# Attention with beacon tokens and an ELU feed-forward: the whole instruction order planned anew, with longer transfers in the head and ring places counted by rows

## The chip, the cores and the metric

The kernel runs on one core of one Trainium2 chip. The metric is the device time in microseconds (us) of one execution, lower is better.

## The reference

Eight batches of eight heads attend causally over 576 tokens plus 16 beacon tokens that every query sees; the result goes, token by token, through a two-layer feed-forward with an ELU between.

```python
B, H, S, Nb, D = (8, 8, 576, 16, 64)          # q, k, v, beacon_k, beacon_v in float32
k_all = np.concatenate([beacon_k, k], axis=2)
v_all = np.concatenate([beacon_v, v], axis=2)
scores = scale * np.matmul(q, k_all.transpose(0, 1, 3, 2))
causal[:, Nb:] = np.triu(np.ones((S, S), dtype=bool), k=1)
scores = np.where(causal, -1000000000.0, scores)
a = np.exp(scores - scores.max(-1, keepdims=True))
a /= a.sum(-1, keepdims=True) + 1e-09
attn_out = np.matmul(a, v_all)
x = attn_out.transpose(0, 2, 1, 3).reshape(B * S, H * D)   # 4608 x 512
h = x @ w_in                                               # w_in: 512 x 2048
g = np.where(h > 0.0, h, np.exp(np.minimum(h, 0.0)) - 1.0)
out = g @ w_out                                            # w_out: 2048 x 512
```

## The kernel before

The attention is cut into 32 pairs of heads: pair n is heads 2hp and 2hp+1 of batch b, with n = 4b + hp. For a pair, scores are made with keys on the partitions (`sc`, L439), exponentiated by ScalarE into fp16 (`et`, L448), masked on the diagonal blocks by GpSimd (L454), and multiplied with v and a column of ones (`av`, L473). VectorE divides by the sums (L488, L489) into `x`. `x` is transposed into `xT`, a ring of four batches, which the feed-forward reads. The feed-forward runs in tiles of tokens: tiles 0, 1 and 2 have 128, 128 and 256 tokens, tiles 3 to 10 have 512. First matmul `hps` (L529), exponential on ScalarE (`e`, L536), clamp on GpSimd (L540), join on VectorE into `gt` (L549), second matmul `ops` (L563), copy (L569), store on SP's queue.

Queries and keys of batches 0 to 2 come in pairs (`load_pair`, 288 KB each, runs of 2304 bytes), are cast to bf16 (`cast_pair`, L323) and transposed by TensorE (`tr`, L388 and L398). From batch 3 on they come by chunks of up to 128 tokens (`load_tok`, runs of 256 bytes), are cast (`cast_tok`, L346) and transposed by DMA on SP's queue (`turn_tok`, L353); from batch 2 on `x` is transposed by DMA too (`turn_x`, L359). v comes in five chunks per batch (`load_v`, L369), 128 rows in four of them and 80 in the fifth, cast by L373. The weights come in four parts each on GpSimd's queue (`load_w`, L380), cast on the way.

All instructions are written out in an order that a planner decides while the program is built (`Plan.run`). Each operation has an engine, a key, a duration that the author assumes, operations that it depends on, and slots that it takes and gives back (buffers, PSUM banks, places in the rings of the DMA queues). The planner steps through time, and on each engine starts the ready operation of the lowest key whose slots are free; the order in which they start is the order of the program. On the chip only the true dependencies, the buffers and the order on each engine are left: an assumed duration, an assumed ring place or a dependency between planned operations sets no wait by itself. Where PE has nothing ready before planned time 30, the planner puts in a filler, a matmul of a constant (`spare`, L274), which the chip then runs whether or not PE would have waited.

`load` plans a transfer: an issue on SP or ScalarE's queue, and an operation on "DMA" of the assumed duration. `place(b, a)` gives the keys of batch b, `FIRST` the order of the first loads by name, `AT0` and `AT` the keys of the steps of a pair, `PACES` and `LAG` those of the tiles, `DMA_AT` and `TOK` the place and the engine of the token casts, `ON_POOL` the engine of the first pair casts, `W_AFTER` the mask after which each weight part is issued.

Of the kernel before, what the change touches and what calls it, by code (L numbers as in the profile page):

```python
# [26 lines left out]
class Plan:  # L27
# [5 lines left out]
    def add(self, *args, **kw):  # L33
        op = Op(*args, **kw)
        self.ops.append(op)
        return op
# [102 lines left out]
def kernel(  # L139
# [35 lines left out]
    kc_sz = [min(P, SK - P * i) for i in range(NKC)]  # L175
# [32 lines left out]
    def blocks_of(groups):  # L208
# [9 lines left out]
            name=nc.get_next_instruction_name(),  # L218
# [43 lines left out]
    with tc.tile_pool(name="psum", bufs=1, space=bass.MemoryType.PSUM) as psum:  # L262
# [21 lines left out]
        def load(key, dur, fn, deps=(), take=(), issue=0.47, units=1, on="SP"):  # L284
            ring = ["ring" + on] * units
            issue = add(on, key, issue, fn, deps=deps, take=take + ring)
            issues[on].append(issue)
            if "vst" not in take and on + str(key) != "ACT-899":
                issues["st"].append(issue)
            return add("DMA", key, dur, None, deps=[issue], lat=2.0, give=ring, queue=0 if on == "SP" else 2, parts=2 * units)  # L290

        v_issue = {}
        issues = {"SP": [], "ACT": [], "st": []}
        add("SP", -1e6, 0.8, None)
        add("ACT", -1e6, 0.8, None)
# [30 lines left out]
        def rows_of(is_k, c):  # L326
            if not is_k:
                return 0, min(P, S - P * c), P * c
            r0 = NB if c == 0 else 0
            return r0, kc_sz[c] - r0, P * c - NB + r0  # L330
# [240 lines left out]
        def do_store(tt, t4, cols):  # L571
# [2 lines left out]

        SHIFT = [-8.8, -12.16, 3.82, 7.68, 7.37, 15.72, 15.25, 20.7]
        AT = [-49.72, -1.57, -0.78, 0.0, 0.42, 1.22, 1.53, -12.56]
        AT0 = [[-47.18, -49.17, -39.96, -41.23], [-43.3, -38.3, -37.64, -35.42], [-44.55, -19.83, -27.66, -35.41]]
        PACES = [(-18.35, 2.5, 7.99, 12.09), (-6.14, 3.4, 55.13, 1.74), (-8.68, 1.33, 24.3, 1.89), (37.46, 1.31, 15.04, 2.29), (75.69, 1.42, 8.27, 3.74), (111.87, 2.41, 34.18, 1.87)]  # L580
        W_AFTER = [[-52.45, -48.57, -122.34, -273.93], [16.05, 17.94, 11.68, 32.16]]
        DMA_AT = [-284.54, -157.9, 350.32]
        TOK = ("001110", "110000", "010101", "111000", "001000")
        ON_POOL = "11110000"
        X_ON_ACT = "00"
        LAG = 17.42
        URGE = -104.22
        Q_ON_ACT = "01101011"
        FIRST = (
            "q2 v0 k2 q1 v6 v9 k1 q3 k3 b1 v8 q6 q4 v1 q5 v7 v3 v2 k4 q7 k5 v5 v4 k7 k6 ").split()  # L590
        ON_ACT = "01"
        V_ON_ACT = "10011110"

        def place(b, a):
            return 32 * (b - 1) + 8 * a + SHIFT[b]

# [3 lines left out]
        w_at, marks = {}, []  # L600
# [7 lines left out]
        def plan_loads(n):  # L608
            b, hp = divmod(n, HP)
            if hp == 0:  # L610
                got = load(load_key(f"b{b}", place(b, 0) - 31), 0.2, partial(load_bk, b), take=["vst"])
                bk_in[b] = add("POOL", place(b, -0.9), 0.6, partial(cast_bk, b),
                               deps=[got] + last_T.get(b - 2, []), give=["vst"])
                if b == 0:
                    marks.append(bk_in[b])
            gots = []
            for is_k in (True, False):
                key = load_key(("k" if is_k else "q") + str(n), place(b, hp) - 30)
                on = "ACT" if n == 0 and not is_k else "SP"
                gots.append(load(key, 0.8, partial(load_pair, n, is_k), take=["st"] if is_k else [], issue=0.61, on=on))  # L620
            eng, dur, on = {
                "0": ("DVE", 0.9, nc.vector), "1": ("POOL", 1.23, nc.gpsimd), "2": ("ACT", 1.35, nc.scalar),
            }[ON_POOL[n] if n < len(ON_POOL) else "1"]
            qk_in[n] = add(
                eng, place(b, hp + AT[0]), dur, partial(cast_pair, n, on), deps=gots + [last_T.get(("pair", n - 2))], take=["sb"], give=["st"])

        last_T = {}

        def plan_v(b):
            for jc in range(NKC):  # L630
                key = load_key(f"v{NKC * b + jc}", place(b - 1, 1.8 + 0.4 * jc))
                on, eng = QUEUES[V_ON_ACT[b] == "1"]
                got = load(key, 1.22 if b < 3 else 1.45, partial(load_v, b, jc, eng), take=["vst"], issue=1.2 if jc == 0 else 0.6, units=8, on=on,
                           deps=v_issue[b - 1] if b > 1 else ())
                v_issue.setdefault(b, []).append(issues[on][-1])
                v_cast[b, jc] = add(
                    "DVE", place(b, -0.7 + 0.16 * jc), 0.56, partial(cast_v, b, jc),
                    deps=[got] + last_AV.get(b - 2, []), give=["vst"])

        def plan_w(which, f4):  # L640
            after = marks[max(0, min(len(marks) - 1, round(W_AFTER[which][f4])))]
            got = add("POOL", after.key + 0.01, 0.8, partial(load_w, which, f4), deps=[after])
# [7 lines left out]
        def plan_tok(b):  # L650
            turned[b] = []
            for is_k in (True, False):
                for c in range(0, NKC, 2):
                    m = min(2, NKC - c)
                    i = (0 if is_k else 0.5) + c // 2
                    on, eng = QUEUES[ON_ACT[not is_k] == "1"]
                    gots = [load(place(b, 0) - 30 + i + 0.01 * j, 1.45, partial(load_tok, b, is_k, c + j, eng), units=8, on=on,
                                 take=["st"] if j == 0 else [], issue=1.2 if is_k and c + j == 0 else 0.65) for j in range(m)]
                    on_dve = TOK[b - PE_B][3 * (not is_k) + c // 2] == "0"
                    cast = add("DVE" if on_dve else "POOL", place(b, DMA_AT[0]) + i, 0.36 * m if on_dve else 0.53 * m,  # L660
                               partial(cast_tok, b, is_k, c, m, nc.vector if on_dve else nc.gpsimd),
                               deps=gots, take=["sb"], give=["st"])
                    for j in range(m):
                        s = add("SP", place(b, DMA_AT[1]) + i, 1.25, partial(turn_tok, b, is_k, c + j),
                                deps=[cast] + last_SC.get(b - 2, []), take=ring4)
                        turned[b].append(add("DMA", place(b, DMA_AT[1]) + i, 0.75, None, deps=[s],
                                             give=ring4 + (["sb"] if j == m - 1 else []), lat=1.0, parts=8))

        def plan_T2(n, key):
# [4 lines left out]
            last_T.setdefault(b, []).append(T)  # L674
            kA = add("DVE", key + 0.4 - URGE, 0.47, partial(do_copy2, n, 0, 0, nc.vector), deps=[T])
            qB = add("ACT", key + 0.4 - URGE, 0.4, partial(do_copy2, n, 1, 1, nc.scalar), deps=[T])
            qA = add("ACT", key + 0.5 - URGE, 0.45, partial(do_copy2, n, 1, 0, nc.scalar), deps=[kA])
# [20 lines left out]
        def plan_pair(n):  # L698
            b, hp = divmod(n, HP)
            at = lambda a: place(b, hp + a)  # L700
            key = AT0[0][hp] - 4 if b == 0 else at(AT[1])
            ready = plan_T2(n, key) if b == 0 else plan_T(n, key) if b < PE_B else turned[b]
            masked = {}
            SC = None
            steps = [((0,), AT0[0][hp]), ((1, 2), AT0[1][hp]), ((3,), AT0[2][hp])] if b == 0 else \
                [((0, 1), at(AT[2])), ((2, 3), at(AT[3]))]
            for units, key in steps:
# [19 lines left out]
            for r, groups in enumerate([(0,), (1,), (2,)] if b == 0 else [(0,), (1, 2)]):  # L727
                key = AT0[r][hp] + 2.4 if b == 0 else at(AT[4 + r])
                us = [u for g in groups for u in CUT.of_range[g]]
# [9 lines left out]
                if b >= XB:  # L739
                    for blk in blks:  # L740
                        part.setdefault(blk, []).append(normed[-1])
                    if hp == HP - 1:
                        for blk in blks:
                            s = add("SP", at(AT[7]), 1.25, partial(turn_x, b, blk), deps=part.pop(blk), take=ring4)
                            turns.append((b, s))
                            done = add("DMA", at(AT[7]), 0.75, None, deps=[s], give=ring4, lat=1.0, parts=8)
                            last_X.setdefault(b, []).append(done)
# [22 lines left out]
        def plan_tile(p):  # L770
            lo, hi = TILES[p]
            base, pitch1, start2, pitch2 = PACES[p] if p < len(PACES) else (32 * (p - 2) + LAG,) + PACES[-1][1:]
            xs = []
# [61 lines left out]
            plan_w(1, f4)  # L835
        for p in range(NTT):
            plan_tile(p)
        for b, s in turns:
            s.deps += readers.get(b - RING // S, [])
        for line in issues.values():  # L840
# [33 lines left out]
```

## Time and profile before

| what | value |
|---|---|
| three runs | 355.54, 355.71, 358.62 us; median 355.71 |
| the profiled execution | 354.51 us, span 352.8 us |
| TensorE busy | 344.7 us (98%), of it fillers 20.5 us |
| VectorE, ScalarE, GpSimd busy | 206.1, 193.6, 180.3 us |
| HBM read, written | 37.22 MB, 9.44 MB |
| first `hps` matmul | 32.34 us after the span's start |

The span is what the profiler saw from the first to the last instruction; the time of the same execution is 1.7 us longer. Busy time counts overlapping matmuls once, and the mean duration of a single matmul is longer than its pace, as matmuls are pipelined. In the chain of waits each step is followed back to what released it. The profile names lines of the program before; in the changed program they lie some lines lower (L439 becomes L442, L529 becomes L532, L563 becomes L566).

### The profile page before, as it was taken

The page shows a single profiled execution, that of the slowest core. Times are in us where ns is not written, and L with a number is a line of the kernel's source. Part 1 is how long each engine was busy: PE and PEld are TensorE (multiplying, and loading weights), DVE is VectorE, ACT ScalarE, POOL GpSimd, SP SyncE. Part 2 cuts the span into 40 slices and gives each one's busy share as a digit, 9 for nine tenths or more (in the row PEclk, how much of TensorE's full clock was granted, in tenths as well). Part 3 has the DMA queues.
Part 4 walks back from the last instruction along what each step waited for, and adds up shares of the span by engine and source line. Part 5 has one row for each costly group of instructions (what it writes and reads, how often), then busy time and mean ns, then how long its engine had stood idle before and what let it go on. Part 6 is the DMA issues. An engine that isn't in the chain of part 4 may idle for free.

```text
span 352.8 us, 8449 instructions
## 1 busy us (share of the span) xinstructions
PE 344.7 (98%) x3299; PEld 195.6 (55%) x3299; DVE 206.1 (58%) x428; ACT 193.6 (55%) x289; POOL 180.3 (51%) x353
## 2 busy tenths in 40 slices
PE   8999999999999999999999999999999999999996
PEld 5668887545555445545476664554445544444444
DVE  1377797567656458456656665664655555455322
ACT  2576887477556746584586547663477443343200
POOL 5587776367635655375476455463554333434200
PEclk9999999999999999999999999999999999999999
DMA  7999996799996979999999669867750220000112
GB/s 196 261 293 224 200 241 114 214 226 153 184 197 132 209 157 186 152 202 189 138 233 167 146 121 240 151 100 187 111 135 32 59 69 32 31 31 32 46 73 91
DMA packets 139480, 52.55 MB, mean 149 GB/s; under 512 B 127536, under 2 KB 131888, under 8 KB 139440
## 3 DMA queue, kind: packets, MB, share of 16 engines
q1 hardware_dynamic: 87472, 35.55, 47.8%
q10 hardware_dynamic: 47744, 12.26, 18.6%
q0 software_dynamic: 4224, 4.19, 7.2%
q8 instruction: 26, 0.43, 0.5%
q14 instruction: 14, 0.11, 0.1%
HBM read 37.22 MB, written 9.44 MB: 132 GB/s over the span
## 4 chain that ended last, share of the span: by engine, by line
PE 82%; DMA 8%; DVE 2%; POOL 2%; ACT 2%; SPq 2%; issue 1%; ACTq 0%; DVEq 0%; POOLq 0%
PE ops L563 31%; PE hps L529 30%; PE av L473 8%; PE sc L439 7%; DMA st<-in_k_dram 3%; PE spare L274 3%; DMA xT<-x 3%; DMA kT<-st 2%; DVE gt L549 1%; PE tr L388 1%; ACT et L448 1%; ACT e L536 1%; POOL e L540 1%; PE xt L499 1%; POOL et L454 1%
## 5 line engine op out<-in xcount | busy, mean ns | idle before, releaser
L563 PE MATMUL ops<-w_out,gt 128*128 128x512 f16 (+1 forms) x592 | 144.2, 374 | 0.2 <-DVE gt L549 0.2
L529 PE MATMUL hps<-xT,w_in 128*128 128x512 f16 (+2 forms) x768 | 141.6, 326 | 1.5 <-DVE xT L510 0.5
L549 DVE SCALAR_TENSOR_TENSOR gt<-e,hps 128x512 f16<-128x512 f32 x144 | 97.5, 684 | 76.6 <-POOL e L540 76.1
L540 POOL TENSOR_SCALAR e<-e 128x512 f32<-128x512 f32 x144 | 88.6, 619 | 99.8 <-ACT e L536 97.6
L536 ACT ACTIVATE e<-hps 128x512 f32<-128x512 f32 x144 | 85.5, 600 | 92.6 <-PE hps L529 87.9
L448 ACT ACTIVATE et<-sc 128x768 f16<-128x768 f32 (+3 forms) x128 | 103.9, 863 | 35.2 <-PE sc L439 31.0
L529 PEld LDWEIGHTS <-w_in 128*128 128x128 f16 x768 | 67.9, 98 | 56.5 <-issue 3.0
L563 PEld LDWEIGHTS <-gt 128*128 128x128 f16 x592 | 54.1, 98 | 57.3 <-issue 3.0
L454 POOL TENSOR_SCALAR_AFFINE_SELECT et<-et 128x256 f16<-128x256 f16 (+2 forms) x160 | 62.1, 414 | 46.5 <-ACT et L448 42.9
L473 PEld LDWEIGHTS <-et 128*128 128x128 f16 (+1 forms) x960 | 35.9, 97 | 10.7 <-issue 2.0
L569 DVE COPY osb<-ops 128x512 f32<-128x512 f32 (+1 forms) x37 | 25.0, 675 | 25.4 <-PE ops L563 24.4
L473 PE MATMUL av<-v,et 128*128 128x65 f16 (+1 forms) x960 | 39.6, 193 | 0.2
L439 PE MATMUL sc<-qT,kT 64*128 64x80 bf16 (+3 forms) x704 | 35.2, 228 | 0.8 <-ACT et L448 0.8
L489 DVE TENSOR_TENSOR x<-av,rl 128x256 f16<-128x256 f32 (+2 forms) x68 | 32.1, 471 | 2.3
L439 PEld LDWEIGHTS <-kT 64*128 64x128 bf16 x704 | 20.7, 95 | 19.9 <-issue 18.1
L373 DVE CAST v<-vst 128x512 f16<-128x512 f32 (+1 forms) x40 | 21.4, 539 | 4.7 <-DMA vst<-in_v_dram 4.7
L488 DVE RECIPROCAL rl<-av 128x4 f32<-128x4 f32 (+2 forms) x68 | 12.4, 182 | 19.8 <-PE av L473 18.9
L274 PE MATMUL spare<-ones 128*128 128x256 bf16 x115 | 20.5, 301 | 1.7 <-DVE ones L812 1.3
L274 PEld LDWEIGHTS <-ones 128*128 128x128 bf16 x115 | 11.1, 107 | 6.9 <-issue 2.2
L346 DVE CAST st<-st 128x1024 bf16<-128x1024 f32 (+2 forms) x18 | 11.4, 643 | 2.1 <-DMA st<-in_k_dram 1.0
L346 POOL CAST st<-st 128x1024 bf16<-128x1024 f32 (+2 forms) x12 | 10.7, 892 | 3.2 <-DMA st<-in_k_dram 2.8
L323 POOL CAST st<-st 128x1152 bf16<-128x1152 f32 x8 | 9.1, 1142 | 4.9 <-DMA st<-in_q_dram 3.4
(35 smaller groups left out, 67.6 us busy)
## 6 DMA issues: line engine op xcount, KB each, us to landing
out_dram<-osb SPq DMA_DIRECT2D x35, 256.0 KB, 2.7
st<-in_q_dram ACTq DMA_DIRECT2D x20, 256.0 KB, 4.2
vst<-in_v_dram ACTq DMA_DIRECT2D x15, 256.0 KB, 4.3
st<-in_k_dram SPq DMA_DIRECT2D x15, 256.0 KB, 5.0
st<-in_k_dram SPq DMA_DIRECT2D x12, 288.0 KB, 7.0
st<-in_q_dram SPq DMA_DIRECT2D x11, 288.0 KB, 6.9
vst<-in_v_dram SPq DMA_DIRECT2D x9, 256.0 KB, 7.1
w_in<-in_moe_w_in_dram POOLq DMA_DIRECT2D x4, 512.0 KB, 12.8
```

Source lines behind the costliest of these rows:

```text
L274: nc.tensor.matmul(out=spare[:, 0:2 * P], lhsT=ones[:, 0:P], rhs=ones, start=True, stop=True)
L439: nc.tensor.matmul(out=sc[:, h, o:o + w], lhsT=kT[D * h:D * h + D, P * jc:P * jc + P], rhs=qT[D * h:D * h + D, q0:q0 + w], start=True, sto ...
L448: nc.scalar.activation(out=et[:, :, 0:w], in_=scs[n, u][:, :, 0:w], func=AFT.Exp, bias=0.0, scale=float(1.0 / (D ** 0.5)))
L454: nc.gpsimd.affine_select(out=et[:, :, c0:c0 + dw], in_=et[:, :, c0:c0 + dw], compare_op=ALU.is_ge, fill=fill0, base=q0 + NB - P * jc, pat ...
L473: nc.tensor.matmul(out=av[:, c:c + D + 1], lhsT=ets[n, CUT.unit_of[jc, at]][0:m, h, col:col + P], rhs=v16[0:m, jc, 2 * hp + h, 0:D + 1], s ...
L489: nc.vector.tensor_tensor(out=x16s[b % 2][:, blks[0]:blks[0] + nb, P * hp:P * hp + P].rearrange("q i (h d) -> q i h d", d=D), in0=av[:, :, ...
L529: nc.tensor.matmul(out=hps[:, o:o + z - a], lhsT=w_in16[:, cc, P * fc:P * fc + P], rhs=xT[cc][:, a % RING:a % RING + z - a], start=(cc == ...
L536: nc.scalar.activation(out=e, in_=hpss[tt, i], func=AFT.Exp, bias=0.0, scale=1.0)
L540: nc.gpsimd.tensor_scalar(out=e, in0=e, scalar1=1.0, scalar2=0.0, op0=ALU.min, op1=ALU.max)
L549: nc.vector.scalar_tensor_tensor(out=gt, in0=es[tt, i], scalar=1.0, in1=hpss[tt, i], op0=ALU.subtract, op1=ALU.max)
L563: nc.tensor.matmul(out=opss[tt, t4][:, cols], lhsT=gts[tt, fc][:, P * t4:P * (t4 + 1)], rhs=w_out16[:, fc, cols], start=(fc == 0), stop=(f ...
L569: nc.vector.tensor_copy(out=osb[:, slice(*cols)], in_=opss[tt, t4][:, slice(*cols)])
```

## The change

`load` gets a list `held`: issues with a key between that of "w0" (or "w1") and the end of `FIRST`, which later depend on the landing of that part of w_in. The assumed time of a pair's load goes from 0.8 to 0.85 us; that of a v chunk from 1.22 (batches 0 to 2) to 1.38 (batches 0 and 1), of 128 rows. v and token chunks take ring places by rows, one for 16, in place of eight each, and their assumed time is scaled with them. All constants of the order are new, `FIRST` among them.

```diff
         def load(key, dur, fn, deps=(), take=(), issue=0.47, units=1, on="SP"):
             ring = ["ring" + on] * units
             issue = add(on, key, issue, fn, deps=deps, take=take + ring)
+            for f4, name in enumerate(HELD):
+                if FIRST.index(name) - 200 < key < len(FIRST) - 200:
+                    held.append((issue, f4))
...
-        v_issue = {}
+        v_issue, held, HELD = {}, [], ("w0", "w1")
...
-        SHIFT = [-8.8, -12.16, 3.82, 7.68, 7.37, 15.72, 15.25, 20.7]
-        AT = [-49.72, -1.57, -0.78, 0.0, 0.42, 1.22, 1.53, -12.56]
-        AT0 = [[-47.18, -49.17, -39.96, -41.23], [-43.3, -38.3, -37.64, -35.42], [-44.55, -19.83, -27.66, -35.41]]
...
-        W_AFTER = [[-52.45, -48.57, -122.34, -273.93], [16.05, 17.94, 11.68, 32.16]]
-        DMA_AT = [-284.54, -157.9, 350.32]
-        TOK = ("001110", "110000", "010101", "111000", "001000")
-        ON_POOL = "11110000"
+        SHIFT = [-8.11, -12.89, 4.08, 7.5, 6.31, 15.87, 19.09, 18.0]
+        AT = [-41.45, -1.77, -0.78, -0.08, 0.42, 1.22, 2.2, -14.13]
+        AT0 = [[-44.86, -49.35, -43.46, -42.7], [-49.19, -42.15, -37.26, -26.77], [-39.84, -19.1, -39.15, -26.7]]
...
+        W_AFTER = [[-29.08, -80.3, -129.97, -296.72], [21.56, 13.65, 16.79, 29.92]]
+        DMA_AT = [-295.03, -105.94, 339.58]
+        TOK = ("001010", "110101", "100010", "110101", "011111")
+        ON_POOL = "01011101"
...
-        LAG = 17.42
-        URGE = -104.22
-        Q_ON_ACT = "01101011"
+        LAG = 14.59
+        URGE = -56.96
+        Q_ON_ACT = "11100000"
         FIRST = (
-            "q2 v0 k2 q1 v6 v9 k1 q3 k3 b1 v8 q6 q4 v1 q5 v7 v3 v2 k4 q7 k5 v5 v4 k7 k6 ").split()
+            "q2 k2 q1 v6 v9 k1 v0 b1 q3 k3 v8 q5 q6 q4 v1 v7 k4 k7 k5 v5 v3 k6 v2 v4 q7 w0 w1 ").split()
...
-                gots.append(load(key, 0.8, partial(load_pair, n, is_k), take=["st"] if is_k else [], issue=0.61, on=on))
+                gots.append(load(key, 0.85, partial(load_pair, n, is_k), take=["st"] if is_k else [], issue=0.61, on=on))
...
-                got = load(key, 1.22 if b < 3 else 1.45, partial(load_v, b, jc, eng), take=["vst"], issue=1.2 if jc == 0 else 0.6, units=8, on=on,
+                units = kc_sz[jc] // 16
+                got = load(key, (1.38 if b < 2 else 1.45) * units / 8, partial(load_v, b, jc, eng), take=["vst"],
+                           issue=1.2 if jc == 0 else 0.6, units=units, on=on,
                            deps=v_issue[b - 1] if b > 1 else ())
...
-                    gots = [load(place(b, 0) - 30 + i + 0.01 * j, 1.45, partial(load_tok, b, is_k, c + j, eng), units=8, on=on,
+                    units = [sum(rows_of(is_k, c + j)[:2]) // 16 for j in range(m)]
+                    gots = [load(place(b, 0) - 30 + i + 0.01 * j, 1.45 * units[j] / 8, partial(load_tok, b, is_k, c + j, eng), units=units[j], on=on,
...
+        for issue, f4 in held:
+            issue.deps.append(w_at[0, 4 * f4])
```

More of the change, by code (lines that the diff above doesn't have):

```diff
@@ L573, in do_store @@
             nc.sync.dma_start(out=out[row:row + P, slice(*cols)], in_=osbs[tt, t4, cols][:, slice(*cols)])
-        SHIFT = [-8.8, -12.16, 3.82, 7.68, 7.37, 15.72, 15.25, 20.7]
-        AT = [-49.72, -1.57, -0.78, 0.0, 0.42, 1.22, 1.53, -12.56]
-        AT0 = [[-47.18, -49.17, -39.96, -41.23], [-43.3, -38.3, -37.64, -35.42], [-44.55, -19.83, -27.66, -35.41]]
-        PACES = [(-18.35, 2.5, 7.99, 12.09), (-6.14, 3.4, 55.13, 1.74), (-8.68, 1.33, 24.3, 1.89), (37.46, 1.31, 15.04, 2.29), (75.69, 1.42, 8.27, 3.74), (111.87, 2.41, 34.18, 1.87)]
-        W_AFTER = [[-52.45, -48.57, -122.34, -273.93], [16.05, 17.94, 11.68, 32.16]]
-        DMA_AT = [-284.54, -157.9, 350.32]
-        TOK = ("001110", "110000", "010101", "111000", "001000")
-        ON_POOL = "11110000"
+        SHIFT = [-8.11, -12.89, 4.08, 7.5, 6.31, 15.87, 19.09, 18.0]
+        AT = [-41.45, -1.77, -0.78, -0.08, 0.42, 1.22, 2.2, -14.13]
+        AT0 = [[-44.86, -49.35, -43.46, -42.7], [-49.19, -42.15, -37.26, -26.77], [-39.84, -19.1, -39.15, -26.7]]
+        PACES = [(-17.99, 4.96, 8.86, 9.41), (-6.14, -3.44, 56.27, 0.45), (-6.33, 1.33, 19.25, 2.21), (37.29, 1.31, 16.39, 2.29), (75.69, 1.42, 7.84, 3.74), (111.96, 2.41, 34.23, 1.87)]
+        W_AFTER = [[-29.08, -80.3, -129.97, -296.72], [21.56, 13.65, 16.79, 29.92]]
+        DMA_AT = [-295.03, -105.94, 339.58]
+        TOK = ("001010", "110101", "100010", "110101", "011111")
+        ON_POOL = "01011101"
         X_ON_ACT = "00"
-        LAG = 17.42
-        URGE = -104.22
-        Q_ON_ACT = "01101011"
+        LAG = 14.59
+        URGE = -56.96
+        Q_ON_ACT = "11100000"
         FIRST = (
-            "q2 v0 k2 q1 v6 v9 k1 q3 k3 b1 v8 q6 q4 v1 q5 v7 v3 v2 k4 q7 k5 v5 v4 k7 k6 ").split()
+            "q2 k2 q1 v6 v9 k1 v0 b1 q3 k3 v8 q5 q6 q4 v1 v7 k4 k7 k5 v5 v3 k6 v2 v4 q7 w0 w1 ").split()
         ON_ACT = "01"
```

## The prediction

> **What bounds the kernel now.** I read the busy rows first, then the slices, the warm-up matmuls by window, the chain of waits around the two ends of the head and in the middle, and the landing times last.
>
> ```profile
> PE 344.7 (98%) x3299; PEld 195.6 (55%) x3299; DVE 206.1 (58%) x428; ACT 193.6 (55%) x289; POOL 180.3 (51%) x353
> ...
> PEclk9999999999999999999999999999999999999999
> DMA  7999996799996979999999669867750220000112
> ```
>
> TensorE is the bound: 98% busy at full clock, no other engine above 58%. But part of that is filler (`spare`, L274), and it all lies in the first 32 us. Columns below: window, its length, PE busy (count), weight-load busy, clock, DMA share, GB/s.
>
> ```profile
> 0.00:8.00 8.00, 6.03 (x32) 4.13 (x33) 1.00 0.73 191
> 8.00:16.00 8.00, 6.20 (x42) 3.46 (x41) 1.00 1.20 269
> 16.00:24.00 8.00, 4.17 (x24) 1.85 (x22) 1.00 1.19 273
> 24.00:32.00 8.00, 4.08 (x21) 1.66 (x21) 1.00 1.19 229
> ```
>
> Four fifths of the head's PE time is filler while the DMA engines are full: the head waits for data. Its end, and a place in the middle, in the chain of waits (start, us, what):
>
> ```profile
> 31.42 0.67 DVE st L323
> 32.09 0.20 DVE xT L510
> 32.34 1.05 PE hps L529 x16
> ...
> 116.94 1.26 SPq L353
> 118.88 5.50 DMA st<-in_k_dram
> 124.37 1.02 POOL st L346
> 126.71 2.97 DMA kT<-st
> ```
>
> The first MoE matmul starts at 32.34 because VectorE cast a later pair before it copied `xT` (0.54 us of PE idle there). From then on PE works almost without a gap; where the chain leaves PE, it goes through SP's queue and the transposing transfers of keys. In the last 70 us PE runs at its pace:
>
> ```profile
> 293.47 0.86 PE ops L563 x4
> 294.33 1.73 PE hps L529 x8
> 334.05 15.59 PE ops L563 x88
> ```
>
> 216 ns per 512 columns, so nothing is to be had there. From starts in the trace I take start-to-start costs: 216 ns per 512 columns, 33 ns per `av`, 56 ns per transpose, 29 to 66 ns per score matmul, 120 ns per warm filler. Laid end to end, the 3299 matmuls give 332.4 us; the span of 352.8 has 1.3 before the first, 3.4 after the last, and 15.7 of waits and cold clock: 6.7 up to 32.34 and 9.0 after it, nearly all before 275 us. All waits over 0.2 us after the first MoE matmul add up to 4.1 us (0.56 at 105.5, 0.61 at 125.9, 0.56 at 147.2, 0.38 at 175.2, 0.60 at 243.7, five smaller 1.4).
>
> **The change, part by part.** The sum is against the profiled execution, 354.5 us with span 352.8; the median of the runs shown, 355.7, lies 1.2 above, and I add that at the end.
>
> *Work.* Comparing the instruction orders: the same matmuls but for 14 more fillers (129 for 115), the same loads, stores and masks; one cast of a pair and five of token chunks go from VectorE to GpSimd. The last 60 blocks on PE are the same. So the end can move only by when the first MoE matmul starts and by the waits behind it: the useful matmuls ahead of that start are 255 now, 254 before.
>
> *The hold is empty.* `held` collects loads with a key above w0's and below the end of `FIRST`. w0 and w1 stand last in `FIRST`, so the only key between is w1's own, and no `load` has that name. No wait is added: cost 0, nothing queued behind it. The new `dur` and `units` alter only the order that is written out; what the rings hold on the chip stays.
>
> *Head, start.* The first pair's cast moves from GpSimd (1137 ns) to VectorE (748 to 919), idle then: its transposes come about 0.3 earlier. Six fewer cold fillers (28 take 5.67 us, 0.2 each) precede them, 20 more warm ones follow at 0.107 to 0.12. PE stands still perhaps 0.7 us before the transposes, as 22 fillers end at about 5.9 and the cast at 6.6. The row: fillers run at 213 ns until 6.12, then at 109.
>
> By the Trainium skill ("TensorE: Matmul & The Clock Gate", Part 1: The HAM clock gate), the warm-up takes about 3.4 us of busy time on a free-running window, not a count of matmuls; by that rule six fillers fewer save no cold time, and a pause inside the window could even delay the switch, which gives the clock rival below.
>
> *Head, body.* Loads are issued in nearly the same order, so landings should hold: the second key load at 8.79, the third at 14.38, the fourth at 16.01. The last three v loads of batch 0 sit later in ScalarE's queue, behind exponentials, by 0.7 to 2 us; SP's loads fill the engines meanwhile, and their casts are ordered behind norms that come later anyway. If that cover is gone, one v cast (0.54) is added. The four w_in transfers follow the same mask as before, which should be about 0.4 earlier (22.1 for 22.5); the first landed at 30.89, so 30.5. After the last filler come 10+10+2+10+10+10+1+14+1+10 matmuls, 2.5 us by the costs above; before, the fillers ended at 29.84 and 2.5 us with the 0.54 wait followed. The `xT` copy now precedes the next kT copy, so that wait goes: −0.5. At the other end, if every wait stays and fillers only add: 20×0.107−6×0.20=+0.9. Fillers stand where PE waited anyway, so I take −0.1.
>
> *Middle.* Attention of later batches starts earlier. PE work between the last scores of batch b−2, which free the kT buffer, and the first scores of b falls from 41.0 to 38.7 us (b=3), 36.5 to 35.7 (4), 41.0 to 38.4 (5), 53.9 to 46.3 (6), 55.6 to 43.6 (7). The needed transposes landed ahead of their score matmul by 3.7, 0.95, 2.1, 13.8 and 13.5 us, which leaves 1.4, 0.15, −0.5, about 6 and 2. SP issues at 1.25 us each; a wait there holds every later load, store and transpose in its queue. For batches 6 and 7 all ten transposes now run ahead of the x transposes: 12.5 us of issue, no longer broken up. I take +0.5 (bounds 0 to +4).
>
> *Tiles.* PE work from the last `av` a tile needs to its first matmul falls from 12.7 to 9.9 us (tile 4), 11.4 to 9.9 (5), 9.8 to 8.9 (6), 8.6 to 6.9 (8), and is 8.1 for 7.7 (7), 6.0 (9). Tile 6 and tile 8 had no reserve. Key loads ahead of batch 2's x transposes now stand together, so SP should be free earlier there: +0.3 (0 to +1.7). Of the old waits (4.1), which this order rearranges, I take 0.4 as gone (0 to 4.1). The moved casts (0.64 us on DVE, 0.89 on POOL) find engines that are busy half the time; without that, 0.25 each, 1.5 in all.
>
> Here a rule speaks against the change. Row: key loads of 256 KB land in 5.0 us and of 160 KB in 4.9 (medians), while the order now counts the small one at 5/8 of the large.
>
> ```profile
> st<-in_k_dram SPq DMA_DIRECT2D x15, 256.0 KB, 5.0
> ...
> st<-in_k_dram SPq DMA_DIRECT2D x5, 160.0 KB, 4.9
> ```
>
> The Trainium skill ("DMA: Bandwidth & Descriptors", Anatomy of one DMA) fits about 2.0 us fixed plus bytes over 436 GB/s on the GpSimd path; by that the small load saves an estimated 0.2 us, not the planned 0.54. The trace agrees that rows hardly count for landing, not with the size of the figures; the sum by it would be some 0.3 higher for each of batches 3 to 5.
>
> *Sum.* −0.1+0.5+0.3−0.4=+0.3: 354.8 on the profiled execution, 356.0 on the median.
>
> **The rivals.** *Faster: the waits go.* The wait at 32 us (0.5) and the 4.1 us behind it vanish, no new ones come: 355.7−4.6=351.1. For it: they are single events at places that the new order rearranges. Against: every gap of the middle but one shrinks.
>
> *Slower: SP's transposes come late.* Place: the first scores of batches 3, 4, 5 and 7. Landings in the trace run from 2.3 to 6.5 us after issue. If the denser bursts land 1.5 us later than before, the reserves 1.4, 0.15, −0.5 and 0.9 (batch 7's last chunk) turn into waits of 0.1+1.35+2.0+0.6=4.05: 355.7+4.05=359.8. It decides from the point where a transpose lands after PE has arrived. For it: batch 4's was within 1 us before. Against: key loads issued side by side may start the chain earlier.
>
> *Fillers count in full.* Every new filler lengthens the head: +0.9, with the other terms 357.0. For it: PE is busy all through the head. Against: DMA is full there.
>
> *The clock.* The pause before the first transposes puts off the switch: some 15 fillers and 20 small matmuls at half pace, 15×0.104+20×0.056=2.7, of which the data wait hides half: 357.3. It is the rule cited above. Against: 4.7 us of fillers precede the pause.
>
> **How the numbers follow.** Forecast (356.0) 0.55; fillers in full 0.10; clock 0.03; faster 0.13; slower 0.19. One per cent, 3.6 us, is about what a measurement of this kernel can tell from no change; forecast, fillers and clock are within it, so faster 0.13, same 0.68, slower 0.19. The range reaches from short of the faster case to just past the slower one, 352.3 to 360.2; the forecast's own is 354 to 358.
>
> **What would show it.** Right: first MoE matmul between 31.7 and 33.3; 129 fillers; PE busy 97 to 98%; single waits of PE of 0.2 to 1 us at the first scores of batch 4 or 5, behind a transpose. Wrong: the start before 31 or after 34; waits behind transposes above 3 us in sum; or no wait over 0.3 us from 60 to 280 us.

## Result, and the profile after

The changed kernel takes 358.82 us (median of 22 runs) against 355.46 us for the kernel before: ratio 1.0088, 95% interval 1.0069 to 1.0107. It is slower by 0.9%; the ratio makes that 3.1 us, the medians 3.4. The forecast was 356.0 in a range of 352.3 to 360.2. The profiled execution took 358.7 us with a span of 357.0 (before: 354.5 and 352.8).

The busy rows and the slices of the kernel after say what those of before said: TensorE bounds it, at full clock.

```profile
PE 346.5 (97%) x3313; PEld 195.8 (55%) x3313; DVE 201.0 (56%) x422; ACT 193.6 (54%) x289; POOL 184.8 (52%) x359
...
PEclk9999999999999999999999999999999999999999
DMA  7999995699798979798987999895521230000022
```

PE is busy 1.8 us longer; the fillers' own busy time grew by 0.6 only (21.1 us for 20.5), since six of those at half pace are gone. The windows over the head (window, length, PE busy, weight-load busy, VectorE, ScalarE, GpSimd, clock, DMA share, GB/s):

```profile
0.00:8.00 8.00, 6.23 (x40) 4.37 (x41) 2.34 (x9) 2.06 (x3) 3.93 (x19) 1.00 0.74 192
8.00:16.00 8.00, 7.62 (x86) 5.39 (x84) 3.87 (x12) 4.78 (x7) 2.92 (x6) 1.00 1.19 260
16.00:24.00 8.00, 8.00 (x97) 5.67 (x97) 3.87 (x14) 4.56 (x8) 5.88 (x12) 1.00 1.19 280
24.00:32.00 8.00, 7.44 (x122) 5.29 (x117) 5.36 (x16) 4.48 (x6) 6.31 (x12) 1.00 1.18 252
```

From 16 to 24 us PE has no free moment: 8.00 of 8.00, fillers included (before: 7.81). That is the row that speaks against "fillers stand where PE waits anyway". The chain of waits at the end of the head (start, us, what):

```profile
29.43 1.13 DVE v L376
...
30.68 0.44 DVE x L492
31.12 0.04 issue
31.16 0.27 PE spare L274
...
33.90 0.61 PE hps L532 x9
```

The wait for `xT` behind the later pair's cast is gone, as the order said. In its place VectorE is held by the cast of v chunk 4, 1.13 us of it in the chain (the cast takes 1.21) where 80x512 elements took 0.41 at 14.95, and with it a norm, the last filler's PSUM bank and all that PE has behind them. The first `hps` starts at 33.83 (its record merges into the last line), 1.5 us later than in the first trace of before. In the middle, the chain has a new kind of step:

```profile
155.83 6.28 DMA st<-in_k_dram
162.11 0.02 issue
162.13 0.69 DVE st L349
...
162.96 0.57 DVE x L492
163.53 0.05 issue
163.58 1.04 PE hps L532 x4
```

A key chunk lands 6.28 us after its issue; its cast stands at the head of VectorE's queue, a norm behind it is late, PE waits 1.07. (In the text a wait of PE counts from where its pace would have had the next matmul; that is 0.16 to 0.17 us more than the idle time in the profile's rows, here 0.91.) PE's waits after the head by the profile (waiting engine and line, what for, us, times, longest):

```profile
PE hps L532 <- DVE gt L552: 1.2, 2, 0.7
PE av L476 <- POOL et L457: 1.2, 1, 1.2
PE hps L532 <- DVE x L492: 0.9, 1, 0.9
PE av L476 <- DVE x L492: 0.6, 1, 0.6
PE av L476 <- DVE gt L552: 0.4, 1, 0.4
```

None is a wait for a transpose of keys at a batch's first scores, which is where I had looked. The three longest, 1.34, 1.07 and 0.90, follow a queue whose head waits for a transfer; they are followed up below. The tail runs at 216 ns per 512 columns, as before:

```profile
329.60 1.73 PE hps L532 x8
...
338.24 15.59 PE ops L566 x88
```

The time can be split at the first `hps` matmul. From there to the start of the last matmul it is 349.36−32.34=317.02 us before and 353.55−33.83=319.72 after. I call these the start and the body: single executions differ by +1.5 and +2.7, the medians by 3.4 in all.

### The profile page after: what moved, and what is told of

It reads as the page before. It is cut to its first block, busy times and chain, and to the rows that moved or that the text cites. A ratio compares the mean times of both kernels' runs of the same rounds, so it can differ in the third digit from the quotient of the medians.

```text
span 357.0 us, 8497 instructions
## 1 busy us (share of the span) xinstructions
PE 346.5 (97%) x3313; PEld 195.8 (55%) x3313; DVE 201.0 (56%) x422; ACT 193.6 (54%) x289; POOL 184.8 (52%) x359
## 4 chain that ended last, share of the span: by engine, by line
PE 78%; DMA 11%; DVE 5%; POOL 2%; issue 2%; SPq 1%; ACT 1%; ACTq 0%; POOLq 0%; DVEq 0%
PE ops L566 31%; PE hps L532 29%; PE av L476 7%; PE sc L442 6%; DMA st<-in_k_dram 3%; DMA vst<-in_v_dram 3%; PE spare L274 2%; DMA kT<-st 2%; DVE gt L552 1%; DMA xT<-x 1%; DMA st<-in_q_dram 1%; POOL et L457 1%; PE tr L391 1%; DVE x L492 1%; DVE v L376 1%
## 5 line engine op out<-in xcount | busy, mean ns | idle before, releaser
L451 ACT ACTIVATE et<-sc 128x736 f16<-128x736 f32 (+3 forms) x128 | 104.3, 864 | 44.7 <-PE sc L442 37.5
L457 POOL TENSOR_SCALAR_AFFINE_SELECT et<-et 128x256 f16<-128x256 f16 (+2 forms) x160 | 60.3, 402 | 51.4 <-ACT et L451 49.5
L476 PE MATMUL av<-v,et 128*128 128x65 f16 (+1 forms) x960 | 40.6, 193 | 2.8 <-POOL et L457 1.2
L274 PE MATMUL spare<-ones 128*128 128x256 bf16 x129 | 21.1, 294 | 1.9 <-DVE ones L818 1.3
L376 DVE CAST v<-vst 128x512 f16<-128x512 f32 (+1 forms) x40 | 20.0, 506 | 2.6 <-DMA vst<-in_v_dram 2.6
L349 POOL CAST st<-st 128x1024 bf16<-128x1024 f32 (+2 forms) x17 | 15.7, 929 | 1.3 <-DMA kT<-st 1.1
L274 PEld LDWEIGHTS <-ones 128*128 128x128 bf16 x129 | 12.4, 105 | 6.7 <-issue 1.4
L326 POOL CAST st<-st 128x1152 bf16<-128x1152 f32 x9 | 10.7, 1194 | 0.5 <-DMA st<-in_k_dram 0.5
L349 DVE CAST st<-st 128x1024 bf16<-128x1024 f32 (+2 forms) x13 | 7.7, 602 | 4.9 <-DMA kT<-st 2.9
```

Source lines behind the costliest of these rows:

```text
L274: nc.tensor.matmul(out=spare[:, 0:2 * P], lhsT=ones[:, 0:P], rhs=ones, start=True, stop=True)
L451: nc.scalar.activation(out=et[:, :, 0:w], in_=scs[n, u][:, :, 0:w], func=AFT.Exp, bias=0.0, scale=float(1.0 / (D ** 0.5)))
L457: nc.gpsimd.affine_select(out=et[:, :, c0:c0 + dw], in_=et[:, :, c0:c0 + dw], compare_op=ALU.is_ge, fill=fill0, base=q0 + NB - P * jc, pat ...
L476: nc.tensor.matmul(out=av[:, c:c + D + 1], lhsT=ets[n, CUT.unit_of[jc, at]][0:m, h, col:col + P], rhs=v16[0:m, jc, 2 * hp + h, 0:D + 1], s ...
```

## The experiments

Theory A: two separate losses, a late start and waits in the body behind queues whose head waits for a transfer. Rivals: B, everything follows from the late start; C, the late start is absorbed; D, waits are only exchanged. The edits act on the list of operations that the planner has put in order: `behind(a, b)` takes a out and puts it after b, `ahead(a, b)` before b. All medians are beside the kernel before on the same chip.

| run | median (before) us | ratio to before, 95% | first hps | body |
|---|---|---|---|---|
| after | 358.82 (355.46) | 1.0088 [1.0069, 1.0107] | 33.83 | 319.7 |
| x1_head_before | 359.74 (356.03) | 1.0096 [1.0064, 1.0129] | 34.62 | 320.3 |
| x2_head_after | 358.02 (356.03) | 1.0055 [1.0028, 1.0083] | 33.35 | 320.0 |
| x3_hold | 361.86 (356.03) | 1.0169 [1.0124, 1.0214] | 35.15 | 321.2 |
| x4_port | 360.32 (356.03) | 1.0111 [1.0077, 1.0146] | 33.22 | 322.0 |
| x5_body | 359.83 (355.40) | 1.0121 [1.0082, 1.0161] | 34.77 | 321.4 |
| x6_fill | 357.47 (355.40) | 1.0051 [1.0024, 1.0077] | 32.46 | 320.6 |
| x7_tok | 357.70 (355.40) | 1.0059 [1.0033, 1.0086] | 34.56 | 318.4 |
| x8_before_again | 355.52 (355.40) | 1.0013 [0.9984, 1.0041] | 32.86 | 317.1 |
| x9_early | 359.19 (355.17) | 1.0111 [1.0079, 1.0142] | 35.15 | 321.3 |
| x10_before_fill | 353.38 (355.17) | 0.9946 [0.9921, 0.9970] | 31.44 | 315.8 |
| x11_best | 355.22 (355.17) | 0.9992 [0.9963, 1.0022] | 31.44 | 317.1 |
| x12_head_fix | 356.71 (354.74) | 1.0056 [1.0025, 1.0086] | 32.37 | 319.7 |

Start and body come from one trace each; the ratios from all runs of a call.

**Splitting head and body: x1_head_before, x2_head_after.**

```diff
-        for _, _, op in order: ...
+        # x1: the operations of before's order up to planned time 40 us, then the rest in after's order
+        # x2: after's order up to 40 us, then the rest in before's
```

> The order of the kernel before up to planned time 40 us (with its 115 fillers, its loads and its engines for the early casts), the order of the kernel after behind that. Theory A (two losses, a late start of about 1.5 us and waits of some 2 us behind queues held by late loads, each on its own): first hps near 32.3, and the median some 1.5 us below the kernel after, about 357.3. Rival B (the late start causes everything; the later waits are its knock-on): as the kernel before, about 355.5. Rival C (PE waits later anyway, so a late start is absorbed): no gain, about 358.8.

> The mirror: the order of the kernel after up to planned time 40 us (129 fillers), the order of the kernel before behind that. Theory A: first hps near 33.8, the waits at 109, 162 and 170 us gone, about 357.0. Rival B: as the kernel after, about 358.8. Rival C: as the kernel before, about 355.5.

Rival B would put x1 at 1.000, rival C would put x2 there; both intervals exclude it. But neither run is a clean split. A spliced order has waits of its own: 2.27 us at 45 us in x1, where the kernel after has 0.65, and 1.70 at 136 in x2. That is why the two do not add up (0.96% and 0.55% against 0.88%). And x1 did not start at 32.3 although its head is the order of before instruction for instruction: the swing of one order, taken up below. With so late a start x1 cannot rule out B; x12 does it better, further down, with the start of before (32.37) and the body of after (319.7).

**The two causes that the first trace suggested: x3_hold, x4_port.**

```diff
+        nc.sync.dma_start(out=late, in_=w_in16[0:1, 0, 0:16])    # x3: gate, late is a scratch tile
+        line.insert(names.index(("load_v", 1, 0)), gate)        # x3
...
+        behind(("do_T", 4), ("do_mm1", 0, 0))                    # x4
+        behind(("cast_pair", 4), ("do_mask", 3, 2, 3, 368, 128)) # x4
```

> The kernel after, with one transfer of 32 bytes on SP's queue ahead of the loads of v5, k6 and q7 that reads the first part of w_in and so holds them until it has landed (what the empty list was for). Theory A: the first part of w_in lands near 30.9 instead of 33.1, since it no longer shares the DMA engines with these three; but the late value cast still ends the fillers near 31.4, so the first hps stays near 33.8 and the time within 0.3 of the kernel after. Rival (the landing is w_in's own affair, its descriptors or its queue): it lands at 33.1 whatever SP does. Rival (w_in alone sets the start): first hps near 32.0 and about 1.5 less.

> The kernel after, with GpSimd's cast of pair 4 moved behind two of its masks (and that pair's transposes behind the first hps block), so that it no longer runs beside VectorE's cast of v chunk 4 of batch 0. Theory A: that cast takes 0.42 us instead of 1.21, the fillers end near 30.5, and PE then waits for w_in, which still lands at 33.1: first hps near 33.2, 0.3 to 0.7 less time. Rival (the two casts only happen to overlap; the long one is long for another reason): it still takes 1.2 us. Rival (the cast alone sets the start): first hps near 32.5 and 1.3 less.

In x3 the first part of w_in landed at 30.80, as theory A had it, and the start did not come earlier. It came at 35.15, 1.3 later than expected, for a reason that lies ahead of the gate: two v casts at 15 us took 1.71 us in this trace (see x8). And its time is not that of the kernel after: the loads behind the gate land from 43.7 us on (v5, k6: 30.7 and 32.2 in the kernel after), and the body is 1.5 us longer. Filled in this way, the list would not have helped.

In x4 the v cast took 0.41 us in place of 1.21, the last filler began at 30.56 (31.16 in the kernel after) and `hps` at 33.22, right behind w_in's landing at 33.17: each as theory A says. The gain was lost in the next step, to my own edit:

```profile
34.88 0.76 DVE kT L452
...
35.83 0.43 DVE x L519
...
36.31 0.29 PE xt L529 x2
```

The late transposes bring their copy `kT` into VectorE's queue ahead of a norm, and PE waits 1.33 us at 35.0.

**Moving four operations of the body: x5_body.**

```diff
+        behind(("load_tok", 4, False, 1), ("do_exp", 13, 1))
+        behind(("load_v", 5, 1), ("do_e", 5, 10))
+        behind(("load_v", 5, 3), ("do_exp", 20, 1))
+        behind(("cast_tok", 5, True, 2, 2), ("do_join", 5, 5))
+        behind(("turn_tok", 5, True, 2), ("cast_tok", 5, True, 2, 2))
```

> The kernel after with four operations moved a few places back in their own queues: three loads on ScalarE (a query chunk of batch 4, v chunks 1 and 3 of batch 5) behind the next one or two exponentials, and one key cast of batch 5 on VectorE behind the next norm and join, with its transpose. Theory A (the waits of 1.34, 1.07, 0.90, 0.25 and 0.25 us at 109 to 179 us come from queues whose head waits for a DMA): these waits go, nothing replaces them, 3 to 3.8 us less, about 355.3. Rival D (waits are exchanged: what is taken from one place comes back at the next, since the four moves make their own loads and casts late): less than 1 us of gain, 358 to 359. Rival B (knock-on of the late start): the waits stay.

The first three are aimed at ScalarE. In the timeline of ScalarE in the kernel after (start, us, what, idle time before it and what ended that):

```profile
109.42 0.38 ACTq L343 DMA_DIRECT2D st<-in_q_dram  x1
109.92 1.70 ACT L451 ACTIVATE et<-sc 128x736 f16<-128x736 f32 x2 [2.43 <-DMA xT<-x]
...
168.90 0.39 ACTq L372 DMA_DIRECT2D vst<-in_v_dram  x1
169.69 0.60 ACT L539 ACTIVATE e<-hps 128x512 f32<-128x512 f32 x1 [3.27 <-PE hps L532]
```

The issue of a query load stands ahead of an exponential and waits until a transpose of `x`, issued at 103.75, lands at 109.40, though the load reads nothing of it: in the program the load waits for a semaphore that is shared with earlier transfers. The exponential, its masks and PE's `av` are late by 1.34 us. In the last two lines a v load holds ScalarE until 168.90 in the same way. With the load moved behind two exponentials this wait is gone in x5, and so is the one of 0.90 at 170. But at the place of the fourth move a new wait came, behind a transpose whose buffer the next cast needs:

```profile
164.49 4.39 DMA kT<-st
...
168.90 0.42 DVE st L379
169.32 0.61 DVE gt L582
```

A wait of 2.68 us at 167 takes the place of what was gained. That the fourth move made it is not shown: the transpose was issued only 0.3 us later than in the kernel after (164.49 for 164.17), but took 4.4 us to land in place of 3.0. After this wait the granted clock was below full, 0.76 from 168 to 172 us and 0.82 from 172 to 176, and the two executions of x5 at the lowest mean clock (0.994 and 0.995) are its slowest, 361.09 and 361.27 us. So theory A holds for the first three moves, the fourth stays open, and the sum is no gain.

**The fillers: x6_fill.**

```diff
+        last = [i for i, n in enumerate(names) if n[0] == "do_fill"][-14:]
+        line = [op for i, op in enumerate(line) if i not in last]
```

> The kernel after without the last 14 of its 129 fillers (those planned from 24.2 to 28.3 us), which makes 115 as before. Theory A (fillers stand where PE waits anyway): within 0.5 of the kernel after. Rival (fillers count in full): 14 x 0.107 = 1.5 less, about 357.3, and the first hps 1.5 earlier.

The rival comes nearer: first `hps` 1.37 us earlier than after, the ratio down from 1.0088 to 1.0051. The difference, 0.0037 or 1.3 us, has an error of 0.0033. A comparison of like with like is x2 and x6, which have the same head but for the 14 fillers and in both of which w_in landed early (30.65, 30.79): 33.35 against 32.46, so 0.9 of the 1.5 us that 14 fillers take. They do not count in full: without them VectorE is the chain at the end of the head, where the same v cast takes 1.21 us from 28.70 on.

**The engines of the token casts: x7_tok.**

```diff
+                on_dve = TOK0[n[1] - 3][3 * (not n[2]) + n[3] // 2] == "0"     # TOK of the kernel before
+                op.fn = partial(op.fn.func, *op.fn.args[:-1], self.eng[not on_dve])
```

> The kernel after, in its own order, with every token cast of batches 3 to 7 on the engine that the kernel before gives it (VectorE or GpSimd). Theory A (the engine of the casts is not what costs): within 0.7 of the kernel after; the waits at 109 and 170 us stay, that at 162 stays too, because the cast in question is on VectorE in both. Rival (the moved casts cost their engines 0.25 each at bad moments): 1 to 1.5 less.

The body is 1.3 us shorter than after's, the ratio lower by 0.0029, with an error of 0.0033. The wait at 109 stays (0.97), that at 170 is gone. Near 164 there is still one of 1.13, but it is another: the key cast of the wait at 162 is on VectorE in the kernel after and on GpSimd in before, against what I had expected, so here it stands at the head of GpSimd's queue (162.39, 1.04 us) and makes a clamp and a `gt` late. The run speaks for the rival, and alone does not prove it: with the casts' engines of after, the body is 319.7 in two traces (after, x12), but 320.6 in x6 and 321.3 in x9.

**How far one order swings: x8_before_again.** The kernel before, unchanged.

> The kernel before, unchanged, for a second trace of it. In the first run here that has its head, first hps was at 34.6 and not at 32.3, with one v chunk landing 1.8 us later. Theory A (the head of the kernel before starts the feed-forward at 32.3 because of its order): 32.3 within 0.5 again. Rival E (the start swings by 1 to 2 us with the landings, and the first trace of before was an early one, its time being 1 us under the median): 33 or later, and then the head's order explains only part of the 1.5 us.

32.86, and a body of 317.1 as in the first trace. The start is 0.52 above the first one, at the edge of theory A and short of rival E's 33. Why x1 swung to 34.6, and x9 to 35.15, is in the chain of x9 (start, us, what):

```profile
5.42 9.64 DMA vst<-in_v_dram
15.09 1.71 DVE v L402 x2
...
16.92 0.43 DVE x L518
```

A v chunk issued at 5.4 lands at 15.07; in the fourteen traces this chunk lands between 13.0 and 15.3. Its cast and the next one on VectorE then meet GpSimd's cast of a pair, and what counts is which cast begins first. In five traces (x1, x3, x5, x9, x12) GpSimd's began 0.04 to 0.33 us before the second v cast, and the two v casts took 1.71 to 1.90 us; in the nine others the second v cast began first, and they took 0.76 to 1.02. The kernel after was on the short side by 0.01 us (14.95 and 14.97). From here on the head is one chain: x3 and x9, which have the head of after but for one issue, start 1.3 us later than it. So the starts of single traces hold a swing of that size, and only the ratios average over it.

**Issuing w_in earlier: x9_early.**

```diff
+        ahead(("load_w", 0, 0), ("do_mask", 1, 0, 0, 0, 112))
```

> The kernel after, with the issue of the first part of w_in moved ahead of the two masks before it on GpSimd, so that it is issued near 20.9 instead of 22.2, ahead of SP's load of v5 (21.9). In the traces so far w_in's first part landed at 30.7 to 31.0 where its issue ended before that of v5, and at 33.1 to 34.5 where it ended after. Theory F (whichever issue ends first is served first): it lands at 31 or before in every run, v5 after it; first hps near 33.3, now set by the fillers and casts, and 0.3 to 0.8 less time, about 358.2. Rival (the landing swings by itself): 33 or later again. Rival G (the two masks put off by 0.9 us make their values late): first hps not earlier, no gain.

With the head so late, the issue fell to 22.20 and not to 20.9. It ended 0.1 us after that of v5, and w_in landed at 33.61. The rule of theory F held, the cure failed. These are the traces in which the two issues end within 0.35 us of each other (issue times and landings from the trace's records, us):

| trace | end of w_in's issue | end of v5's issue | w_in lands | v5 lands |
|---|---|---|---|---|
| x6 | 22.79 | 22.94 | 30.79 | 33.86 |
| x2 | 22.64 | 22.83 | 30.65 | 33.78 |
| x8 | 23.95 | 24.05 | 30.95 | 34.65 |
| before | 23.43 | 23.70 | 30.89 | 34.10 |
| x9 | 23.11 | 23.01 | 33.61 | 30.42 |
| x4 | 23.08 | 22.98 | 33.17 | 31.49 |
| after | 23.11 | 22.92 | 33.13 | 30.67 |
| x7 | 23.23 | 22.90 | 34.52 | 31.33 |

**Putting it together: x10_before_fill, x11_best, x12_head_fix.**

```diff
+        behind(("cast_pair", 5), ("do_xcopy", 1, (1,)))     # x10, in the order of the kernel before
+        line = ... without the last 30 fillers              # x10, x11, x12
+        ahead(("load_w", 0, 0), ("do_mask", 1, 0, 0, 0, 112))    # x11, x12
+        the three moved loads of x5, and the casts of x7         # x11
```

> The kernel before without its last 30 of 115 fillers (those planned from 18.1 us on), and with the cast of pair 5 behind the xT copy that PE waits for (0.54). If fillers count in full from about 18 us on, as 14 of them did in the kernel after, w_in's landing (30.9) bounds the first hps: 31.0 to 31.3 instead of 32.3 to 32.9, and 1 to 1.5 less than the kernel before, about 354.2. Rival (the clock or the landings take it back): no gain, 355 to 356, or the granted clock falls under 1.0 before 32 us.

> The kernel after with all that has helped: without its last 30 fillers, the first w_in part early, the three loads of ScalarE moved back, and the token casts on the engines of the kernel before. Theory A (the losses are separate and add up: fillers 1.3, engines of the casts 1.1, ScalarE's loads 1.0, w_in 0.5): 3 to 4 less than the kernel after, 354.8 to 355.8, level with the kernel before. Rival D (waits are exchanged): 356.5 or more.

> The kernel after with the two cures of the head alone: without its last 30 fillers, and with the first w_in part issued ahead of two masks. The casts' engines and ScalarE's loads stay as in the kernel after. With x11_best it splits the 3.6 us between head and body. Theory A (about two thirds of the loss come from the head): first hps near 31.4, 2.0 to 2.4 less than the kernel after, 356.4 to 356.8; what is then left to x11_best, 1.2 to 1.6, is the body's. Rival C (a late start is absorbed): 358 or more, all of the gain of x11_best is the body's. Rival B (everything comes from the start): 355.2, as x11_best.

x10 beats both kernels: 353.38 us, 0.5% under the kernel before, by its two edits together, which were not run apart. The first `hps` is at 31.44, 0.4 us behind w_in's landing (31.07). Part of the rival came too: PE was busy only 1.28 and 1.21 of the 2 us windows before 28 us, and then the granted clock (the number behind GpSimd's) fell:

```profile
24.00:26.00 2.00, 1.28 (x23) 0.85 (x20) 1.26 (x6) 1.74 (x3) 2.00 (x5) 1.00 1.15 320
26.00:28.00 2.00, 1.21 (x25) 0.91 (x27) 1.79 (x6) 1.03 (x2) 2.00 (x5) 1.00 1.20 204
28.00:30.00 2.00, 2.00 (x34) 1.94 (x34) 1.24 (x3) 0.84 (x1) 1.99 (x5) 0.61 1.21 196
30.00:32.00 2.00, 2.00 (x37) 1.79 (x35) 1.93 (x9) 1.10 (x2) 1.53 (x3) 0.54 1.22 197
```

x11, with 14 fillers more, kept 1.00. In x10 nine of the eleven executions have a mean clock of 0.995 or less; the two at 1.000 took 351.49 and 352.00 us, less than any of the nine. A few fillers between 22 and 28 us may thus be worth keeping; that was not tried. x11 brings the order of the kernel after level with the kernel before (ratio down by 0.0096, error 0.0035), as theory A had summed it. But part of that is a gain that the order of before can have too: against x10, which has the same first `hps` (31.44), x11 is still slower by 0.0046 (error 0.0038), 1.6 us. The waits of PE that are left in it after 33 us:

```profile
PE hps L571 <- DVE gt L591: 1.0, 3, 0.5
PE av L515 <- DVE x L531: 0.6, 1, 0.6
PE av L515 <- DVE gt L591: 0.6, 2, 0.4
PE hps L571 <- DMA xT<-x: 0.5, 1, 0.5
```

The waits behind a held exponential (`POOL et`) and a held norm ahead of `hps` are not among them. x12 has the head's cures alone: a third of the gain in ratio (0.0032, error 0.0036) where two thirds were expected, with the body unchanged at 319.7. Its start, 32.37, missed the 31.4 expected: the two v casts at 14 us took 1.90 us in this trace. The other 0.0064 (error 0.0042) belong to ScalarE's loads and the casts' engines together; the bodies say the same, 319.7 and 317.1. A start as early as that of before with the body of after is also what rules out rival B.

## Why the prediction was right or wrong

**Size and sign.** +0.3 was forecast; +4.2 came between the two profiled executions and +3.4 between the medians. That is still within about one per cent, the likeliest case, and inside the range, but by the width of the range and not by the sum: one term of the head has the wrong sign, and the body lost by a mechanism that has no term. As far as the sum goes, the hit is luck.

**Head, start: right.** The first transposes start at 6.33 in place of 6.93, and no clock was lost: fillers at half pace end at 5.3 in place of 6.1, in spite of a pause of 0.5 us before the transposes.

**Head, body: −0.1 predicted; +1.5 between the first traces, +1.0 against the second trace of before. This step failed, in three places.** First, "Fillers stand where PE waited anyway". The upper end given there, +0.9, was nearer, and the rival "fillers in full" had the right mechanism, if not in full (0.9 of 1.5 for the last 14). The working also took fillers for four fifths of the head's PE time; they are 20.5 of 29.8 busy us, two thirds, so PE had more work of its own between them. The profile of before showed it, in the chain between the two ends at which I read it:

```profile
14.28 1.52 PE spare L274 x11
15.80 0.11 PE xt L499 x2
15.91 0.43 PE spare L274 x3
```

From 14 to 30.6 us the chain is PE itself, fillers and all; a filler in the chain of waits delays what stands behind it until another engine takes over the chain. Second, "so 30.5" for w_in: the issue was 0.3 earlier, as said, but SP's load of v5 was earlier by 0.8 and got in front. I moved the landing with its own issue and did not ask which transfer would stand ahead of it. In the trace of after this cost nothing yet, as w_in landed at 33.13 and the work ahead of `hps` ran to 33.83; it bounds the start in x4 (33.17 and 33.22). Third, the cover of the v casts: "one v cast (0.54) is added" named the right work and half of its price, 1.13, since GpSimd now casts pair 4 at the same moment. The cast that was moved off VectorE came back as a longer cast on it.

The row for this: v casts with no GpSimd work beside them take 0.41 to 0.43 us, beside a pair's cast that began first up to 1.38. The Trainium skill ("SBUF — State Buffer", Who interferes with whom) says that VectorE, in the modes that use both its ports (a cast can be in one), and GpSimd share a pair of ports, and that the one that issues first holds it for its whole instruction. The trace agrees: GpSimd's cast ends at 30.27, so waiting it out would give an estimated 0.92+0.42=1.34 for the cast that began at 29.35; 1.21 was measured. The other way round, in the kernel after GpSimd's cast that began at 14.97, just behind a v cast, took 1.40 us where 1.14 is usual.

**Hold: right that it holds nothing.** x3 adds that holding, done as it was there, would not have paid.

**Middle: +0.5 predicted at the first scores of batches 3 to 7, 0 measured there.** The landings had reserve enough in the end, and the rival of late transposes fell with it. The same 200-odd us lost time through a mechanism that I had no term for: loads and casts at the head of an in-order queue.

**Tiles, old waits, casts: +0.3−0.4 predicted.** The old waits did go, more than I took: none of the five single ones of 0.38 to 0.61 us is left. New ones came: 0.65, 0.55, 1.34, 0.25, 0.78, 1.07, 0.90, 0.25 and 0.21, 6.0 in sum, so +1.9 of the body's +2.7; the rest is not accounted for. The price that I set aside, "0.25 each, 1.5 in all" for the moved casts, is what x7 measures (1.3 in the body, 1.0 in the median), within its error.

**The price of a load by rows.** The medians to landing (queue, count, size, us), which in the trace of before spoke against counting rows, moved:

```profile
st<-in_k_dram SPq DMA_DIRECT2D x15, 256.0 KB, 4.5
...
st<-in_k_dram SPq DMA_DIRECT2D x5, 160.0 KB, 3.6
```

0.9 us between the sizes here, 0.1 before. The difference lies in what else is in flight; neither trace gives a price for rows, and no wait could be put down to it.

**What would show it.** 129 fillers and PE at 97% came as said; the start at 33.83 fell between "right" (to 33.3) and "wrong" (from 34); single waits of 0.2 to 1.3 us came, but not at first scores behind a transpose.

**Still open.** How the 1.3 us of x7 spread over single casts; the waits of 0.65, 0.55 and 0.78 near 45, 55 and 139 us, which stayed in every kernel with after's body and which no run took away; and the 1.6 us by which x11 is still behind x10.

## What to carry to other kernels

Read the chain of waits through its whole length before pricing a filler, and move a landing only after asking what else is issued within a microsecond of it. In an order written out by hand, look for loads that stand ahead of compute on an engine's queue: an issue that must wait holds the engine, and the fix is to place it behind the next work that is ready, provided that nothing behind it needs its buffer. One trace of a head swings by over 1 us with which of two casts begins first, so a second trace of the same kernel is worth a run.

## What the runs showed of the hardware

Two transfers issued 0.1 to 0.3 us apart on different queues landed in the order in which their issues ended, in all eight traces of the table; the loser landed 1.7 to 3.7 us after the winner. A cast of 80x512 elements on VectorE took 1.35 to 1.38 us when GpSimd's cast of 128x1152 had begun 0.04 to 0.33 us before it, and 0.41 to 0.63 when it began first, in all fourteen traces. An unrelated landing (`xT`, 5.65 us after its issue) held ScalarE for 2.43 us through the issue of a load. With PE busy 62% of 4 us (24 to 28 us of x10), the clock fell to 0.61 and 0.54 in the next windows, with no pause of PE over 0.82 us; with 80% of them (x11) it did not. That is one trace of each; in x5 it fell behind a single pause of 2.52 us (0.76 from 168 to 172 us).
